# Turning the second half's attention probabilities by 64-row products, behind the whole dense sum, with half of the probabilities in the norm tile

## The chip, the cores and the metric

The kernel runs on one core of one Trainium2 chip. The metric is the device time in microseconds (us) of one execution. The engines are named as in the profile: PE is the matmul engine (TensorE), PEld its weight load, DVE the vector engine, ACT the scalar engine, POOL the GpSimd engine, SP the engine that issues most DMAs.

## The reference

Four layers stand one behind the other on a sequence of 2048 tokens of width 512: a recurrent attention layer A, a dense layer B, A again, B again, each with a residual sum and a layer norm ahead of it. In short:

```python
def attention(x, mem0):                     # A, 32 heads of 128
    mem = mem0                              # 8 memory rows
    for s in range(64):                     # segments of 32 tokens
        h = concat(mem, x[32*s:32*s+32])    # 40 rows
        q, k, v = h @ Wq, h @ Wk, h @ Wv    # per head
        scores = where(mask, q @ k.T * 128**-0.5, -1e9)
        o = (softmax(scores) @ v) @ Wo      # summed over the heads
        mem = o[:8]                         # carried to the next segment
        out[s] = o[8:]

x = x + attention(layernorm(x), mem0)
x = x + relu(layernorm(x) @ w1) @ w2        # B, inner width 1376
x = x + attention(layernorm(x), mem0)
x = x + relu(layernorm(x) @ w1) @ w2
```

Weights and inputs are bf16. The recurrence makes the segments of one attention layer strictly sequential.

## The kernel before

**Steps.** The program is a row of 68 steps, `step(k)` for k = 1 to 67 behind `first_step()` (k = 0). In step k the first attention layer (a = 0) works on segment k and the second attention layer (a = 1) on segment k - 4; from k = 4 to 63 both are active ("two-layer steps", 60 of them), in the others one ("single" steps: 0 to 3 and 64 to 67). The dense layer of a segment pair runs inside the later steps as `dense_h` (first product and ReLU) and `dense_y` (second product, "the dense sum", accumulated in the PSUM bank `sp_banks[1]`).

**Order.** PE, DVE, SP and POOL run in the order in which the program is written (`tc.manual_schedule`); ACT's order is made by a planner. PE and DVE take their instructions strictly in that order, so a product or a copy that must wait holds up all that stands behind it on its engine. The framework puts in the semaphore waits, from the tiles that an instruction reads and writes.

**A step.** With L = 40 rows per layer, the 32 heads are worked in two halves (`hf` = 0, 1) of 16. For each half: queries and keys (`qk`, L591, evicted from PSUM by L597 on ACT and L599 on DVE), scores (L625) into `sp`, and `softmax`: maximum (L643), difference (L647), exponential (L649, on ACT), sum (L659), reciprocal (L660) and the product with it (L664), which writes the probabilities. A row of the probability tile is (head parity g, query), a column (head pair, layer, key). To be multiplied with the values they have to be turned, keys onto partitions.

- Half 0 lies in `P_sb` and is turned by a transposing DMA into `PT0` (`turn_p`, L682).
- Half 1 lies in `P1_sb` and is turned on PE by `transpose_p(1, cut)`: for each of 8 head pairs and each layer a product of all 128 rows, 64 columns of `P1_sb` held, 80 columns of the identity moving (L675), into two PSUM tiles `tp`. The first tile (`cut` = 5 pairs in two-layer steps, 4 in single ones) is copied to `PT_sb` by ACT, the second by DVE (L679).

After it come `weighted_v` (L701, 64 small products of a 40-row value block with the turned probabilities, the first 32 of them with half 0), the copies of its result to `OTm` (memory rows) and `OTx` (tokens) (`outputs`, L719), the product of the memory rows with `Wo` (`output_mem`, L633), the new memory (L849, L857, L868, L872), values of the next step (L354, L797).

**Around the change.** In a two-layer step the order on PE behind the second half's scores is: filling work (`dense_h`, `block`), `dense_y(k-2, 0, 9)` (18 products), `transpose_p(1, 5)` (16), `dense_y(k-2, 9, 11)` (4), `weighted_v`, `output_mem`. On DVE it is: sums, reciprocals and L664 of the second half, `add_output(k-1)` (two sums into the residual, L379; in every fourth step there is none, and a short piece of the input's moments, L220 and L221, may stand in its place), then the copy of the second `tp` (L679), then the copies L719.

**The norm tile.** `XN` (128 x 512, bf16) takes the normalised rows at the end of a step (L227). A transposing DMA (`transpose_step`, L291) turns it into `xnT` early in the next step; nothing else reads it, but for the last rows of the program.

Of the kernel before, what the change touches and what calls it, by code (L numbers as in the profile page):

```python
# [7 lines left out]
BF = mybir.dt.bfloat16  # L8
F32 = mybir.dt.float32
ALU = mybir.AluOpType  # L10
# [12 lines left out]
def kernel(  # L23
# [14 lines left out]
    nc = tc.nc  # L38
    _, S, Dm = A_x.shape
    _, H, Dh = A_Wq.shape[0], A_Wq.shape[1], A_Wq.shape[2]  # L40
# [4 lines left out]
    L = M + SEG  # L45
    NSEG = S // SEG
    assert NSEG % 4 == 0 and DELTA == 4
    LAST = NSEG + DELTA - 1
    NXT = NSEG // 4
    NC4 = Dm // 128  # L50
    NFC = (Dff + 127) // 128
# [5 lines left out]
    const = ctx.enter_context(tc.tile_pool(name="const", bufs=1))  # L57
    wk = ctx.enter_context(tc.tile_pool(name="wk", bufs=2))
    dram = ctx.enter_context(tc.tile_pool(name="vdram", bufs=2, space=DRAM))
    ps_c = ctx.enter_context(tc.tile_pool(name="ps_c", bufs=3, space=PSUM))  # L60
# [11 lines left out]
    def has1(k):  # L72
        return DELTA <= k <= LAST
# [22 lines left out]
    def span(d):  # L96
        offs = ([0] if has0(d) else []) + [o for o, _ in slots_of.get(d, [])]
        return base(d) + min(offs), base(d) + max(offs) + 32
# [65 lines left out]
    ident = const.tile([128, 128], BF)  # L164
# [3 lines left out]
    ident_q = ident[:].rearrange("p (g q) -> p g q", g=2)[:, :, 0:L]  # L168
# [22 lines left out]
    XN = const.tile([128, Dm], BF)  # L191
# [3 lines left out]
    Vs = const.tile([128, H * Dh], BF)  # L195
    P_sb = const.tile([128, 8, 128], BF)
    nc.gpsimd.memset(P_sb[:], 0.0)
    P1_sb = const.tile([128, 16 * L + 24], BF)
    nc.gpsimd.memset(P1_sb[:], 0.0)
    PT_sb = const.tile([128, 8, 2, L], BF)  # L200
    PT0 = const.tile([128, 8, 128], BF)
    OTx = const.tile([128, H, 64], BF)
# [6 lines left out]
    for a in range(2):  # L209
        t = ps_s.tile([128, 512], F32, name=f"sp{a}")  # L210
# [24 lines left out]
    def moments_x(n):  # L235
        return stat_tail(stats_x(n), "x")
# [295 lines left out]
    def dense_y(d, f0, f1, bank=1):  # L532
        if not 0 <= d <= LAST:
            return
        lo, hi = span(d)
        n = hi - lo
        for fc in range(NFC)[f0:f1]:
            fs = 128 if fc < NFC - 1 else F_LAST
            for j in range(2):


                w = 8 * L if fc == 0 else 256
                nc.tensor.matmul(sp_banks[bank][64 * j:64 * j + n, 0:w], lhsT=hT_tiles[d][0:fs, fc, 0:n],  # L543
                                 rhs=w2_flat[0:fs, fc * Dm + 256 * j:fc * Dm + 256 * j + w],
                                 start=(fc == 0), stop=(fc == NFC - 1), skip_group_check=True,
                                 tile_position=(0, 64 * j))
# [68 lines left out]
    def masks(*act):  # L615
        for a in act:
            nc.vector.tensor_copy(out=sp_tiles[a], in_=maskb2)  # L617
# [20 lines left out]
    def exponentials(act):  # L638
        mxs, ess = {}, {}
        for a in act:  # L640
            sp = sp_tiles[a]
            mxs[a] = wk.tile([128, 8], F32, tag="mx", bufs=2, name="mx")
            nc.vector.tensor_reduce(out=mxs[a][:], in_=sp, axis=AX.X, op=ALU.max)  # L643
        for a in act:
            sp = sp_tiles[a]
            es = ess[a] = wk.tile([128, 8, L], F32, tag="es", bufs=2, name="es")
            nc.vector.tensor_tensor(out=es[:], in0=sp, in1=mxs[a][:].unsqueeze(2).to_broadcast([128, 8, L]),  # L647
                                    op=ALU.subtract)
            last_exp[0] = nc.scalar.activation(out=es[:], in_=es[:], func=ACTF.Exp, scale=SCALE)  # L649
        return ess  # L650

    def softmax(hf, act, by_pe=False, ess=None):
        if ess is None:
            ess = exponentials(act)
        if by_pe and hf:
            transpose_p(0)
        for a, es in ess.items():
            sm = wk.tile([128, 8], F32, tag="sm", bufs=2)
            nc.vector.tensor_reduce(out=sm[:], in_=es[:], axis=AX.X, op=ALU.add)  # L659
            nc.vector.reciprocal(out=sm[:], in_=sm[:])  # L660
            eng = nc.vector if by_pe or (hf, a) == (1, act[-1]) else nc.gpsimd
            P = P1_sb[:, 0:16 * L].rearrange("p (s a q) -> p s a q", s=8, a=2)[:, :, a, :] if hf else \
                P_sb[:, :, 64 * a:64 * a + L]
            eng.tensor_tensor(out=P, in0=es[:],  # L664
                              in1=sm[:].unsqueeze(2).to_broadcast([128, 8, L]), op=ALU.mult)

    def transpose_p(hf, cut=4):

        for s0, ns, copy in ((0, cut, nc.scalar.copy), (cut, 8 - cut, nc.vector.tensor_copy)):
            tp = ps_c.tile([128, ns, 2, L], F32, tag="c", name="tp")  # L670
            for sl in range(ns):
                for a in range(2):
                    c = L * (2 * (s0 + sl) + a)
                    P = P1_sb[:, c:c + 64] if hf else P_sb[:, s0 + sl, 64 * a:64 * a + 64]
                    nc.tensor.matmul(tp[64 * a:64 * a + 64, sl], lhsT=P, rhs=ident_q,  # L675
                                     start=True, stop=True, tile_position=(0, 64 * a))
            PT = PT_sb[:, s0:s0 + ns] if hf else \
                PT0[:, s0:s0 + ns].rearrange("p s (g q) -> p s g q", g=2)[:, :, :, 0:L]
            copy(out=PT, in_=tp[:])  # L679

    def turn_p():
        nc.sync.dma_start_transpose(out=PT0[:], in_=P_sb[:].rearrange("p s k -> p (s k)"))  # L682
# [3 lines left out]
    def weighted_v(act):  # L686
        pvs = {}
        for t, (h0, nh) in enumerate(PVS):
# [6 lines left out]
            for hi in range(nh):  # L695
                hf, hh = divmod(h0 + hi, 16)
                sl, g2 = divmod(hh, 2)
                for a in act:
                    R = 64 * a
                    PT = PT_sb[R:R + L, sl, g2, :] if hf else PT0[R:R + L, sl, 64 * g2:64 * g2 + L]  # L700
                    nc.tensor.matmul(pvs[t, a][:, hi, :], lhsT=Vs[R:R + L, (h0 + hi) * Dh:(h0 + hi + 1) * Dh],  # L701
                                     rhs=PT, start=(hi == 0 or (t, a) != (1, 1)), stop=True,
                                     skip_group_check=(t, a) == (1, 1))
# [181 lines left out]
    def first_step():  # L885


        slots = iter([w1_flat[:, 512 * i:512 * i + 512] for i in range(NC4 * Dff // 512)] +
                     [w2_flat[:, 512 * i:512 * i + 512] for i in range(8)])
        masks(0)  # L890
        with tc.high_priority(offset=PRIO):
            qks = qk(0, [0])
            scores(qks, [0])
            softmax(0, [0], True)
            values_first(0)
            memory_values(0, (next(slots), None), (0,))
            values_second(0, next(slots))
            values0(1, 0, stage=next(slots))
            values0(1, 2, stage=next(slots))
            m = moments_x(2)  # L900
            normalize(nc.vector, xbs[2], xbs[2], m, 0, 128)
            inputs_T(2)
            values0(3, 0, stage=next(slots))
            values0(3, 2, stage=next(slots))
            load_x(1)
            qks = qk(1, [0], between=lambda: values0(5, 0, stage=next(slots)))
            scores(qks, [0])
            softmax(1, [0], True)
            values0(5, 2, stage=next(slots))
            values_first(1)  # L910
            memory_values(0, (None, next(slots)), (1,))
            transpose_p(1)
            tokens_in(1)
            nc.gpsimd.tensor_copy(out=HTm[:, :, 2 * M:32], in_=spare_T(1))
            values_second(1, next(slots))
            pvs = weighted_v([0])
            outputs(0, pvs)
            wo = ps_wo.tile([128, Dm], F32, tag="wo", name="wo")
            for groups, heads in zip((((1, 4),), ((1, 6),), ((3, 4),), ((3, 6), (5, 4)), ()), WO_PARTS):
                for p, n in groups:  # L920
                    values0(p, n, stage=next(slots))
                output_mem(0, wo, *heads)
            new_memory(0, [0], wo)
            output_ride(0)
            prepare(1)
# [7 lines left out]
    def step(k):  # L933
        act = layers(k)
        single = len(act) == 1
# [4 lines left out]
        ahead = has1(k + 1) or not cont  # L940
# [65 lines left out]
        else:  # L1006
# [1 line left out]
                evict_behind.append(last_exp[0].ins)  # L1008
            block(k, part, H)
            evict_behind.clear()  # L1010
        f_mid = 9 if ahead or k == 2 else 5
        if k < LAST:
            dense_y(k - 2, 0, f_mid)
        if not single:
# [5 lines left out]
        elif not single and k % 4 == 1 and has_x:  # L1020
            mom["x"] = stat_tail(mom["stats"], "x")
        with tc.high_priority(offset=PRIO):
            transpose_p(1, 4 if single else 5)
        if ahead and k < LAST:
            dense_y(k - 2, f_mid, NFC)
        tokens_in(k + 1)
        if k < LAST and spare_T(k + 1) is not None:
            nc.gpsimd.tensor_copy(out=HTm[:, :, 2 * M:32], in_=spare_T(k + 1))
# [11 lines left out]
        if cont:  # L1040
            with tc.high_priority(offset=PRIO):
                pool, tag = (ps_c, "c") if single else (ps_wo, "wo")
# [24 lines left out]
    with tc.manual_schedule(engines={mybir.EngineType.PE, mybir.EngineType.DVE, mybir.EngineType.SP,  # L1067
                                   mybir.EngineType.Pool}):
        load_rest()
        tp = transpose_pe(mem0)  # L1070
# [21 lines left out]
        R = residual(d)  # L1092
        t = xnT_tiles[d + 2] = wk.tile([128, NC4, 128], BF, tag="xnT", bufs=1, name="xnT")
# [8 lines left out]
        for fc in order:  # L1102
            fs = 128 if fc < NFC - 1 else F_LAST
            for q in range(4):
                u, j = divmod(q, 2)
                nc.tensor.matmul(sp_banks[0][32 * q:32 * q + 32, 0:256], lhsT=hT_tiles[d][0:fs, fc, SEG * u:SEG * u + SEG],  # L1106
                                 rhs=w2_flat[0:fs, fc * Dm + 256 * j:fc * Dm + 256 * j + 256],
                                 start=(fc == order[0]), stop=(fc == order[-1]), tile_position=(0, 32 * q))
        ob = wk.tile([128, 256], BF, tag="xb", bufs=1, name="ob")
        nc.vector.tensor_tensor(out=ob[:], in0=R[:, 0:256], in1=sp_banks[0][:, 0:256], op=ALU.add)  # L1110
        for u in range(2):
            r = S - SEG * (u + 1)
            for j, queue in ((0, nc.sync), (1, nc.scalar)):
                q = 64 * u + 32 * j
# [36 lines left out]
```

## Time and profile before

| what | value |
|---|---|
| runs | 1577.96, 1580.86, 1581.55 us; median 1580.86 us |
| profiled execution | span 1580.0 us from the first to the last instruction; the page gives no other time of it |
| busy, share of the span | PE 98%, PEld 81%, DVE 81%, ACT 47%, POOL 22% |
| granted PE clock | 1.000 |
| mean length of a two-layer step | 23.09 us |

The span of the profiled execution is 0.86 us below the median of the runs, so the two can be compared nearly without a correction. In the rows of the profile, "L675" is line 675 of the kernel, `out<-in` are the program's names with numbers left out (`P_sb` stands for `P1_sb` as well), x16 is a number of instructions, and `[0.75 <-ACT HTm L868]` is idle time of the engine ahead of the row and what ended it. A matmul's duration (some 0.18 us) is its latency; products follow each other at a far shorter distance, which is read from the starts of rows.

### The profile page before, as it was taken

How to read it: one execution, taken by the hardware profiler on the slowest of the kernel's cores; microseconds unless marked ns; L12 is line 12 of the kernel's file. 1: busy time of each engine (PE TensorE's matmuls, PEld its weight loads, DVE VectorE, ACT ScalarE, POOL GpSimd, SP SyncE). 2: the span in 40 equal slices, each digit the busy share in tenths (PEclk: the TensorE clock that was granted, in tenths of full speed). 3: DMA queues.
4: the chain of work that ended last, by engine and by line, in shares of the span. 5: the costliest groups of instructions: out<-in, count | busy, mean ns of one | idle time of the engine just before them, and what ended most of it. 6: DMA issues, size and time to landing. Idle time of an engine off the chain costs nothing. (4 is left out here: it accounts for less than half of the span.)

```text
span 1580.0 us, 95139 instructions
## 1 busy us (share of the span) xinstructions
PE 1548.6 (98%) x42866; PEld 1286.3 (81%) x42866; DVE 1277.3 (81%) x3300; ACT 734.7 (47%) x1762; POOL 349.8 (22%) x670
## 2 busy tenths in 40 slices
PE   5899999999999999999999999999999999999998
PEld 3677888888888888888888888988888898888876
DVE  3578888888888888888888888888888888887866
ACT  3435445454544545454454545445454544545433
POOL 2012122222222222222122222212222221222110
PEclk9999999999999999999999999999999999999999
DMA  9734432434353244434433343443443344333331
GB/s 369 246 77 76 87 84 78 81 92 79 78 92 84 78 82 94 80 76 91 84 80 80 99 80 76 88 84 79 77 99 77 72 87 80 82 74 95 75 69 41
DMA packets 222021, 146.26 MB, mean 93 GB/s; under 512 B 123464, under 2 KB 215984, under 8 KB 221616
## 3 DMA queue, kind: packets, MB, share of 16 engines
q1 hardware_dynamic: 218448, 135.96, 38.8%
q8 instruction: 336, 5.51, 1.5%
q0 software_dynamic: 3072, 4.20, 1.1%
q14 instruction: 69, 0.57, 0.1%
q10 hardware_dynamic: 96, 0.03, 0.0%
HBM read 65.41 MB, written 45.35 MB: 70 GB/s over the span
## 5 line engine op out<-in xcount | busy, mean ns | idle before, releaser
L597 ACT CAST QT<-qp 128x480 bf16<-128x480 f32 (+3 forms) x408 | 201.5, 494 | 433.4 <-PE qp L591 433.1
L591 PE MATMUL qp<-HT,Wq_sb 128*128 128x80 bf16 (+1 forms) x8704 | 371.3, 200 | 3.2 <-POOL HT L786 1.2
L591 PEld LDWEIGHTS <-Wq_sb 128*128 128x128 bf16 x8704 | 325.9, 100 | 35.2 <-issue 27.5
L591 PE MATMUL qp<-HT,Wk_sb 128*128 128x80 bf16 (+1 forms) x8704 | 347.3, 199 | 1.7 <-issue 1.3
L591 PEld LDWEIGHTS <-Wk_sb 128*128 128x128 bf16 x8704 | 319.5, 100 | 2.6 <-issue 1.6
L664 POOL TENSOR_TENSOR P_sb<-es,sm 128x320 bf16<-128x320 f32 x185 | 130.8, 721 | 714.8 <-ACT QT L597 299.4
L599 DVE CAST KT<-qp 128x480 bf16<-128x480 f32 (+3 forms) x408 | 220.3, 565 | 36.3 <-PE qp L591 32.9
L643 DVE TENSOR_REDUCE mx<-sp 128x8 f32<-128x320 f32 x256 | 115.1, 487 | 133.1 <-PE sp L625 130.9
L373 PE MATMUL wox<-Wo_sb,OTx 128*64 128x256 bf16 x2880 | 173.6, 273 | 0.0
L373 PEld LDWEIGHTS <-OTx 128*64 128x64 bf16 x2880 | 150.2, 110 | 2.9
L649 ACT ACTIVATE es<-es 128x320 f32<-128x320 f32 x256 | 109.5, 468 | 61.9 <-DVE es L647 61.0
L797 PE MATMUL vm<-Wv_sb,HTm 128*32 128x512 bf16 x2176 | 129.4, 379 | 1.8 <-DVE KT L599 1.0
L354 PE MATMUL v<-Wv_sb,xnT 128*32 128x512 bf16 x2048 | 128.8, 378 | 0.0
L633 PE MATMUL wo<-Wo_sb,OTm 128*32 128x512 bf16 x2144 | 128.6, 380 | 0.0
L659 DVE TENSOR_REDUCE sm<-es 128x8 f32<-128x320 f32 x256 | 117.4, 459 | 13.5 <-ACT es L649 5.0
L617 DVE CAST sp<-maskb 128x320 f32<-128x320 bf16 x256 | 118.3, 483 | 0.0
L647 DVE TENSOR_TENSOR es<-sp,mx 128x320 f32<-128x320 f32 x256 | 113.6, 482 | 1.5
L543 PE MATMUL sp<-w_sb,hT 128*64 128x256 bf16 (+4 forms) x1452 | 103.9, 276 | 0.4 <-issue 0.4
L522 PE MATMUL hp<-xnT,w_sb 128*128 128x64 bf16 (+1 forms) x2948 | 98.5, 192 | 0.9 <-issue 0.5
L801 ACT CAST VmS<-vm 128x512 bf16<-128x512 f32 x134 | 78.5, 586 | 44.4 <-PE vm L797 42.5
L222 POOL TENSOR_TENSOR mv<-mv,mhalf_t 128x1 f32<-128x1 f32 x82 | 45.8, 558 | 224.6 <-DVE mv L221 218.9
L797 PEld LDWEIGHTS <-HTm 128*32 128x32 bf16 x2176 | 54.7, 97 | 48.8 <-issue 3.1
(125 smaller groups left out, 2088.5 us busy)
## 6 DMA issues: line engine op xcount, KB each, us to landing
Vs<-vd SPq DMA_DIRECT2D x96, 256.0 KB
vd<-vst SPq DMA_DIRECT2D x181, 128.0 KB
vmd<-VmS SPq DMA_DIRECT2D x134, 128.0 KB
Vs<-vmd SPq DMA_DIRECT2D x254, 32.0 KB
Vs<-vmd SPq DMA_DIRECT2D x60, 128.0 KB
Wq_sb<-in_A_Wq_dram SPq DMA_DIRECT2D x2, 2048.0 KB
Wk_sb<-in_A_Wk_dram SPq DMA_DIRECT2D x2, 2048.0 KB
Wv_sb<-in_A_Wv_dram SPq DMA_DIRECT2D x2, 2048.0 KB
```

The lines of the kernel that those rows point to most:

```text
L354: nc.tensor.matmul(vp[32 * j:32 * j + 32, :], lhsT=tokens[:, c4, :], rhs=Wv_sb[:, c4, n * 512:(n + 1) * 512], start=(c4 == 0), stop=(c4 == ...
L373: nc.tensor.matmul(out[64 * j:64 * j + nr, 0:256], lhsT=lhsT, rhs=rhs[:, 256 * j:256 * j + 256], start=start, stop=stop, tile_position=(0, ...
L591: nc.tensor.matmul(qp[:, hi, 0:ncol], lhsT=W_sb[:, c4, h * Dh:(h + 1) * Dh], rhs=HT[:, c4, a_lo:a_hi, :], start=(c4 == 0), stop=(c4 == NC4 ...
L597: nc.scalar.copy(out=dst[:, 0:nh, a_lo * L:a_hi * L], in_=qp[:, 0:nh, 0:ncol])
L599: nc.vector.tensor_copy(out=dst[:, 0:nh, a_lo * L:a_hi * L], in_=qp[:, 0:nh, 0:ncol])
L617: nc.vector.tensor_copy(out=sp_tiles[a], in_=maskb2)
L633: nc.tensor.matmul(wo[32 * j:32 * j + 32, :], lhsT=OTm[:, h, n, 2 * M * c:2 * M * c + 4 * M], rhs=Wo_sb[:, h, :], start=(h < 4), stop=(h > ...
L643: nc.vector.tensor_reduce(out=mxs[a][:], in_=sp, axis=AX.X, op=ALU.max)
L647: nc.vector.tensor_tensor(out=es[:], in0=sp, in1=mxs[a][:].unsqueeze(2).to_broadcast([128, 8, L]), op=ALU.subtract)
L659: nc.vector.tensor_reduce(out=sm[:], in_=es[:], axis=AX.X, op=ALU.add)
L664: eng.tensor_tensor(out=P, in0=es[:], in1=sm[:].unsqueeze(2).to_broadcast([128, 8, L]), op=ALU.mult)
L797: nc.tensor.matmul(vp[32 * j:32 * j + 32, :], lhsT=HTm[:, c4, :], rhs=Wv_sb[:, c4, n * 512:(n + 1) * 512], start=(c4 == 0), stop=(c4 == NC ...
```

## The change

- The second half's probabilities are laid out as 4 head pairs of 104 columns (layer 0 in columns 0 to 39, layer 1 in 64 to 103) in each of two tiles: pairs 0 to 3 (u = 0) in the norm tile `XN`, pairs 4 to 7 (u = 1) in `P1_sb`. The product L664 of this half becomes two products of 128 x 160 per layer, on the same engine as before (POOL for layer 0 of a two-layer step, else DVE).
- `transpose_p(1, cut)` is replaced by `turn_second`: for u, pair and head parity g a product over the 64 rows of that g, 104 columns held, 40 columns of the identity moving, so that both layers come out at once. The result of g lies in PSUM tile `tps[g]`. Behind the 8 products of u = 0, ACT copies `tps[0]`'s and DVE `tps[1]`'s columns of u = 0 to `PT_sb`, then the 8 products of u = 1 go into the other columns of the same two tiles, and are copied in the same way.
- All 22 products of the dense sum stand ahead of the turn, where 4 of them stood behind it (in steps 3 to 66).

```diff
-    P1_sb = const.tile([128, 16 * L + 24], BF)
+    PW1 = 64 + L
+    P1_sb = const.tile([128, 4 * PW1], BF)
     nc.gpsimd.memset(P1_sb[:], 0.0)
+    P1 = [t[:, 0:4 * PW1].rearrange("p (s k) -> p s k", s=4) for t in (XN, P1_sb)]
...
             eng = nc.vector if by_pe or (hf, a) == (1, act[-1]) else nc.gpsimd
-            P = P1_sb[:, 0:16 * L].rearrange("p (s a q) -> p s a q", s=8, a=2)[:, :, a, :] if hf else \
-                P_sb[:, :, 64 * a:64 * a + L]
-            eng.tensor_tensor(out=P, in0=es[:],
-                              in1=sm[:].unsqueeze(2).to_broadcast([128, 8, L]), op=ALU.mult)
+            if not hf:
+                eng.tensor_tensor(out=P_sb[:, :, 64 * a:64 * a + L], in0=es[:],
+                                  in1=sm[:].unsqueeze(2).to_broadcast([128, 8, L]), op=ALU.mult)
+                continue
+            for u in range(2):
+                eng.tensor_tensor(out=P1[u][:, :, 64 * a:64 * a + L], in0=es[:, 4 * u:4 * u + 4],
+                                  in1=sm[:, 4 * u:4 * u + 4].unsqueeze(2).to_broadcast([128, 4, L]), op=ALU.mult)
+
+    def turn_second():
+
+        tps = [ps_c.tile([128, 8, L], F32, tag="c", name="tp") for _ in range(2)]
+        for u in range(2):
+            for sl in range(4):
+                for g in range(2):
+                    R = 64 * g
+                    nc.tensor.matmul(tps[g][0:PW1, 4 * u + sl, :], lhsT=P1[u][R:R + 64, sl, :],
+                                     rhs=ident[R:R + 64, R:R + L], start=True, stop=True)
+            for g, copy in ((0, nc.scalar.copy), (1, nc.vector.tensor_copy)):
+                copy(out=PT_sb[0:PW1, 4 * u:4 * u + 4, g, :], in_=tps[g][0:PW1, 4 * u:4 * u + 4, :])
...
-        f_mid = 9 if ahead or k == 2 else 5
+        f_mid = NFC if ahead else 9 if k == 2 else 5
         if k < LAST:
             dense_y(k - 2, 0, f_mid)
...
         with tc.high_priority(offset=PRIO):
-            transpose_p(1, 4 if single else 5)
-        if ahead and k < LAST:
-            dense_y(k - 2, f_mid, NFC)
+            turn_second()
         tokens_in(k + 1)
```

`transpose_p` itself stays, without its `hf` and `cut`, for the first half of the three steps that turn it on PE (0, 1 and 67).

More of the change, by code (lines that the diff above doesn't have):

```diff
@@ L655, in softmax @@
         if by_pe and hf:
-            transpose_p(0)
+            transpose_p()
         for a, es in ess.items():
@@ L661, in softmax @@
             eng = nc.vector if by_pe or (hf, a) == (1, act[-1]) else nc.gpsimd
-            P = P1_sb[:, 0:16 * L].rearrange("p (s a q) -> p s a q", s=8, a=2)[:, :, a, :] if hf else \
-                P_sb[:, :, 64 * a:64 * a + L]
-            eng.tensor_tensor(out=P, in0=es[:],
-                              in1=sm[:].unsqueeze(2).to_broadcast([128, 8, L]), op=ALU.mult)
[L667 to L671, printed above, removed]
+            if not hf:
+                eng.tensor_tensor(out=P_sb[:, :, 64 * a:64 * a + L], in0=es[:],
+                                  in1=sm[:].unsqueeze(2).to_broadcast([128, 8, L]), op=ALU.mult)
+                continue
@@ L672, in transpose_p @@
+    def transpose_p():
+        for s0, copy in ((0, nc.scalar.copy), (4, nc.vector.tensor_copy)):
+            tp = ps_c.tile([128, 4, 2, L], F32, tag="c", name="tp")
+            for sl in range(4):
                 for a in range(2):
-                    c = L * (2 * (s0 + sl) + a)
-                    P = P1_sb[:, c:c + 64] if hf else P_sb[:, s0 + sl, 64 * a:64 * a + 64]
-                    nc.tensor.matmul(tp[64 * a:64 * a + 64, sl], lhsT=P, rhs=ident_q,
+                    nc.tensor.matmul(tp[64 * a:64 * a + 64, sl], lhsT=P_sb[:, s0 + sl, 64 * a:64 * a + 64], rhs=ident_q,
@@ L676, in transpose_p @@
                                      start=True, stop=True, tile_position=(0, 64 * a))
-            PT = PT_sb[:, s0:s0 + ns] if hf else \
-                PT0[:, s0:s0 + ns].rearrange("p s (g q) -> p s g q", g=2)[:, :, :, 0:L]
-            copy(out=PT, in_=tp[:])
+            copy(out=PT0[:, s0:s0 + 4].rearrange("p s (g q) -> p s g q", g=2)[:, :, :, 0:L], in_=tp[:])
     def turn_p():
@@ L911, in first_step @@
             memory_values(0, (None, next(slots)), (1,))
-            transpose_p(1)
+            turn_second()
             tokens_in(1)
@@ L1022, in step @@
         with tc.high_priority(offset=PRIO):
-            transpose_p(1, 4 if single else 5)
-        if ahead and k < LAST:
-            dense_y(k - 2, f_mid, NFC)
+            turn_second()
         tokens_in(k + 1)
```

## The prediction

> **What bounds the kernel now.** I read the page first, then the timeline of one two-layer step around the turn, then the same distances for all 60 of them, then the groups by shape, and last the tiles that two engines share.
>
> ```profile
> PE 1548.6 (98%) x42866; PEld 1286.3 (81%) x42866; DVE 1277.3 (81%) x3300; ACT 734.7 (47%) x1762; POOL 349.8 (22%) x670
> ```
>
> PE is busy 98% of the span at a granted clock of 1.000; its 31 us of idle time lie mostly at the two ends of the run. In the middle a step is a gapless row of products, so an added wait on PE costs its full length in every step, and a product saved gains its distance to the next one. The timeline around one turn:
>
> ```profile
> 818.33 0.71 POOL L664 TENSOR_TENSOR P_sb<-es,sm 128x320 bf16<-128x320 f32 x1 [3.74 <-DVE sm L660]
> ...
> 818.55 1.18 PE L543 MATMUL sp<-w_sb,hT 128*64 128x320 bf16 x18
> 818.77 0.63 DVE L664 TENSOR_TENSOR P_sb<-es,sm 128x320 bf16<-128x320 f32 x1
> 819.43 0.85 DVE L379 TENSOR_TENSOR R<-R,wox 64x256 f32<-64x256 f32 x2
> 819.56 0.46 PE L675 MATMUL tp<-ident,P_sb 128*64 128x80 bf16 x16
> 819.85 0.39 PE L543 MATMUL sp<-w_sb,hT 128*64 128x256 bf16 x4
> 819.95 0.49 ACT L679 CAST PT_sb<-tp 128x400 bf16<-128x400 f32 x1 [2.17 <-PE tp L675]
> 820.17 0.49 PE L701 MATMUL pv<-PT,Vs 40*128 40x40 bf16 x25
> 820.31 0.41 DVE L679 CAST PT_sb<-tp 128x240 bf16<-128x240 f32 x1
> ...
> 820.59 0.18 PE L701 MATMUL pv<-PT_sb,Vs 40*128 40x40 bf16 x1
> ...
> 820.67 0.73 DVE L719 CAST OTm<-pv 128x96 bf16<-128x96 f32 x3
> ...
> 821.08 0.61 PE L633 MATMUL wo<-Wo_sb,OTm 128*32 128x512 bf16 x8
> ```
>
> From the starts: the 16 products of the turn take 0.29 us of PE, the 4 of the dense sum 0.32, the 64 of L701 0.91 with the hand-over to L633. The last 4 dense products and the 32 products with half 0 (820.17 to 820.59) cover the copies of `tp`: ACT's ends at 820.44, DVE's, late because the sums L379 keep DVE until 820.28, at 820.72, and it is first needed at the 21st product with half 1, about 820.84. No PE time is lost here today.
>
> The rows that price the new operations:
>
> ```profile
> L599 DVE CAST KT<-qp 128x160 bf16<-128x160 f32 x16 | 5.0, 315 | 0.1
> L597 ACT CAST QT<-qp 128x160 bf16<-128x160 f32 x16 | 4.7, 293 | 17.1 <-PE qp L591 17.1
> L701 PE MATMUL pv<-PT_sb,Vs 40*128 40x40 bf16 x1536 | 37.3, 177 | 0.0
> ```
>
> And one place where two engines share a PSUM tile, in a single step (timeline):
>
> ```profile
> 1512.95 0.27 PE L857 MATMUL mt<-sel,wm 128*32 128x16 bf16 x16
> 1513.66 0.19 ACT L868 CAST HTm<-mt 128x32 bf16<-128x32 f32 x1
> 1513.88 0.19 DVE L872 CAST HT<-mt 128x32 bf16<-128x32 f32 x1 [0.75 <-ACT HTm L868]
> ```
>
> Both only read `mt`, and write different tiles; yet DVE, idle for 0.75 us, waits for ACT's end and starts 0.03 us later. The view of L872 has this wait 5 times of 5, and where DVE copies first (all two-layer steps), ACT starts 0.10 to 0.14 us behind DVE's end in all 60. So accesses of different engines to one PSUM bank are put one after the other here, even where the data would not ask for it.
>
> **The change, part by part.** Times run from the start of the new turn, T'.
>
> *Dense sum moved.* The 4 products cost the same 0.32 us ahead of the turn, so T' is 0.32 us later than the old start (819.88 in the step shown). The probabilities are ready earlier than that (DVE's L664 ends at 819.40). Nothing is gained or lost on PE, but the cover behind the turn is gone: its price stands below.
>
> *Turn's products.* 16 of 40 moving columns over 64 rows, alternating between row halves, for 16 of 80 columns. Nearest rows: L701 (64 such alternating products in 0.81 us, 12.6 ns each) and L625 (32 products of 40 columns in about 0.5 us, 16 ns). So 0.20 to 0.27 us; I take 0.20, as L701 has the same row split. Gain 0.08 us a step, at most; at the other end 0.02.
>
> *Probabilities in two pieces.* DVE's 128x320 product takes 0.63 us. For two halves the bounds are nothing more, or one more fixed part: casts of 160 and 320 columns (315 and 485 ns) leave 145 ns fixed. Neighbours on DVE overlap by 20 to 90 ns, so I take +0.10, between 0 and 0.14. It delays `add_output` and the copies behind it in DVE's queue, not the turn. On POOL the one product (0.71 us) becomes two; even at twice the time it ends at 819.77, before T'. Behind it stand the token copies (L786, L1028), which the next step needs 6 us later: nothing. `XN` was last read by the transposing DMA that feeds `dense_h`, whose products ran 4 us before, and is next written at the end of the step: nothing.
>
> *The wait inside the turn.* The products of u = 1 write the same two PSUM tiles, other columns, that ACT and DVE are reading for u = 0. By the `mt` rows PE must wait for both copies. The 8th product starts at T'+0.09 and its data are there at +0.27 (177 ns). ACT is idle (2.17 us before its copy now), starts at +0.31, and ends at +0.60. DVE's copy takes 0.315 us and starts at +0.32 if DVE is free, else behind `add_output`. In the step shown add_output ended 0.72 us behind the old turn's start, so at 0.72 - 0.32 + 0.10 = +0.50; copy from +0.53 to +0.84; PE goes on at +0.89 (0.05 us is what PE takes behind DVE in the rows of `P_sb` and `KT`). In steps where it ended at 0.59 the same sum gives +0.77, where there is no `add_output` +0.69. Then 0.10 for u = 1, and L701 starts at +0.99, +0.87 or +0.79, against +0.29 today (820.17 less 819.88). So 0.70, 0.58 and 0.50 us a step. 28 steps are of the first kind, 13 of the second, some 15 of the third, the rest between; applied to the recorded end of DVE's work in each of the 60, the mean is 0.61 us. The turn's 0.08 is in this.
>
> *Behind the turn.* The copies of u = 1 end 0.65 us after PE resumes on them; L701 needs them 0.70 us after: no further wait. DVE's first copy L719 then ends at about 0.90, and L633 follows it by 0.14: 1.04, against 1.01 if L701 alone set it: +0.02 a step.
>
> *Single steps.* The same wait with DVE free costs about 0.4 us in each of 8, but in one (1527) L701 already waits 0.9 us for the DMA of `PT`, and hides it: 2.8 us.
>
> Sum: 60 x 0.63 + 2.8 = 40.6 us. On the execution's 1580.0 us that is 1620.6; carried to the median of the runs, 1621 us. Low end: P halves free, nothing behind the turn, 60 x 0.54 + 2 = 34.5, so 1615. High end: P halves at +0.14, 16.7 ns a product, a release that takes 0.15 us (the distance from DVE's L719 to L633), 0.1 us behind: 60 x 0.88 + 4 = 57, so 1638.
>
> *Two rules of the Trainium skill.* "PSUM — Partial Sum Buffer", section "PSUM bank collisions raise a hardware error", says that a PE write and a read by ACT or DVE in one bank and the same partitions collide even at disjoint columns, and that software has to keep them apart; this speaks against the change, and by it neither of the first two rivals below could happen. The `mt` rows show such keeping apart for two readers; no row shows it for a PE write. "TensorE: Matmul & The Clock Gate", section "LDWEIGHTS (loading the stationary operand)", makes a weight load's time its columns over 1.2: 87 ns for 104 columns, 53 for 64. By it the sum would be up to 33 us larger (16 x 34 ns x 60), if loads were exposed. The trace doesn't bear it out: 128x64 loads take 111 ns, 40x128 loads 93 ns.
>
> **The rivals.** *Copies only late, no wait inside the turn*: if the framework lets u = 1 run beside the copies, L701 starts at +0.21 and meets its first product with half 1 of g = 1 at +0.61, when DVE's copy is at +0.84, +0.72 or +0.65. With the release and the late L719 copies behind them this costs 0.28, 0.15 and 0.08 us: about 12 us, 1593. For it: probabilities of the two layers are written into one SBUF tile by POOL and DVE at the same time (818.33 and 818.77), so disjoint parts are told apart there. Against it: `mt`.
>
> *Faster*: the same, and L701 never waits. That is 60 x 0.075, 4.5 us less, 1576. It decides from where both copies of u = 0 are done by +0.56, and DVE's of u = 1 by +0.8. ACT's alone ends at +0.60 by its row and DVE's, when free, at +0.64, so it would need copies a fifth faster and DVE free of L379.
>
> *Loads exposed*: the turn's loads don't overlap, at 93 ns each (L701's loads) for 16 instead of 12.6: 1.3 us a step, 77 us on top, 1698. Against it: L701's 64 loads of 128 columns lie inside 0.81 us.
>
> *It doesn't do what it says*: the turn's products are no shorter (0.27), and the waits are covered by later slack, so the time stays. Against it: PE has no idle time in the steps that could take up 0.6 us.
>
> **How the numbers follow.** The forecast has 0.86, late copies alone 0.07, faster 0.03, exposed loads 0.02, no change 0.02. A measurement of this kernel can tell about 0.2%, 3.2 us, from no change. Faster is thus 0.03, same 0.02, slower 0.95. The forecast's own range is 1615 to 1638; to hold 8 in 10 with its unknown sizes it is stretched down to the late-copies case: 1592 to 1638.
>
> **What would show it.** In the profile after: the 16 products of the turn in two groups of 8, 0.6 to 0.8 us apart, with PE idle between them, released by L679 of DVE (in most steps) or ACT; some 0.5 us of idle PE at each turn; a two-layer step of 23.7 us instead of 23.09; four L679 copies a step near 0.3 us; L701 behind the turn without a wait. Wrong: the second group right behind the first (then the late copies, seen as waits at L701's products with `PT_sb`), or loads of 104 columns that push the products to 50 ns and more apart.

## The result and the profile after

The changed kernel takes 1639.86 us (median of 5 runs, 1638.81 to 1641.69) against 1580.86 us before: a ratio of 1.0377, 95% interval 1.0364 to 1.0389. That is 59 us more, where 40 were forecast, and 1.9 us above the end of the range. The profiled execution took 1638.81 us, with a span of 1637.1 us, 57.1 more than the span before, at the same granted clock of 1.000. The page of after:

```profile
PE 1579.0 (96%) x42866; PEld 1317.0 (80%) x42866; DVE 1305.6 (80%) x3436; ACT 741.8 (45%) x1830; POOL 358.6 (22%) x730
```

PE has as many instructions as before, but is now idle for 58 us instead of 31. The view of the waits says at what (us in total, times, longest):

```profile
PE tp L679 <- ACT PT_sb L682: 25.8, 68, 0.6
```

L679 is the turn's product, L682 its copies: 68 waits, one in each step, that were not there before. The same turn as the one shown of before, in the timeline of after:

```profile
846.02 0.44 POOL L669 TENSOR_TENSOR XN<-es,sm 128x160 bf16<-128x160 f32 x1 [3.80 <-DVE sm L662]
846.40 0.33 DVE L669 TENSOR_TENSOR XN<-es,sm 128x160 bf16<-128x160 f32 x1
846.44 0.60 POOL L669 TENSOR_TENSOR P_sb<-es,sm 128x160 bf16<-128x160 f32 x1
846.64 0.57 DVE L669 TENSOR_TENSOR P_sb<-es,sm 128x160 bf16<-128x160 f32 x1
...
847.25 0.85 DVE L381 TENSOR_TENSOR R<-R,wox 64x256 f32<-64x256 f32 x2
847.51 0.37 PE L679 MATMUL tp<-ident,XN 64*104 64x40 bf16 x8
847.91 0.29 ACT L682 CAST PT_sb<-tp 104x160 bf16<-104x160 f32 x1 [2.49 <-PE tp L679]
848.14 0.33 DVE L682 CAST PT_sb<-tp 104x160 bf16<-104x160 f32 x1
848.26 0.58 PE L679 MATMUL tp<-ident,P_sb 64*104 64x40 bf16 x8 [0.38 <-ACT PT_sb L682]
848.68 0.55 PE L714 MATMUL pv<-PT,Vs 40*128 40x40 bf16 x25
...
848.90 0.32 DVE L682 CAST PT_sb<-tp 104x160 bf16<-104x160 f32 x1 [0.44 <-PE tp L679]
...
849.24 0.56 DVE L732 CAST OTm<-pv 128x96 bf16<-128x96 f32 x2
...
849.64 0.40 PE L635 MATMUL wo<-Wo_sb,OTm 128*32 128x512 bf16 x4
```

The two groups of 8 are 0.75 us apart. The first product of the second group starts 0.05 us behind ACT's copy, the second one, at 848.51, 0.05 us behind DVE's (848.14 + 0.33), which came late because the residual sums L381 kept DVE until 848.10. From the turn's start to L635 it is 2.13 us, where the step before had 1.52 with 4 products of the dense sum inside. Two steps' lengths, from turn to turn, before and after (the first two numbers of a row, window and length):

```profile
819.56:842.65 23.09, 23.09 (x651) 19.80 (x648) 19.61 (x51) 10.60 (x25) 5.34 (x11) 1.00 0.37 82
842.65:865.73 23.08, 23.08 (x651) 19.81 (x648) 19.27 (x50) 10.59 (x25) 5.35 (x11) 1.00 0.38 82
```

```profile
847.51:871.66 24.15, 23.69 (x649) 20.24 (x648) 20.15 (x53) 10.75 (x26) 5.46 (x12) 1.00 0.45 78
871.66:895.56 23.90, 23.52 (x649) 20.23 (x648) 19.70 (x52) 10.69 (x26) 5.47 (x12) 1.00 0.45 80
```

For the account I took the starts of the rows in all 60 two-layer steps and averaged the **stage** from the first product of the dense sum to the first of the output product (L633, here L635):

| kernel | to the turn | turn, first to last product | to the first value product | to the output product | stage |
|---|---|---|---|---|---|
| before | 1.025 | 0.259 | 0.360 | 0.916 | 2.56 us |
| after | 1.326 | 1.050 | 0.045 | 1.000 | 3.42 us |

60 x 0.861 = 51.7 us of the 57.1 lie in this stage. From the first query product of one step to that of the next, the two-layer steps last 23.07 us in the mean before (the 23.09 given above is the median) and 23.95 after, so some 1.5 us lie in the rest of these steps and 3.9 in the single steps with the start and the end. A price of its own for keeping half of the probabilities in the norm tile can't be seen: the rest of a two-layer step is only 0.025 us longer.

### The profile page after: what moved, and what is told of

Read it like the earlier page. It is cut to its first block, busy times and chain, and to the rows that moved or that the text cites. A ratio compares the mean times of both kernels' runs of the same rounds, so it can differ in the third digit from the quotient of the medians.

```text
span 1637.1 us, 95522 instructions
## 1 busy us (share of the span) xinstructions
PE 1579.0 (96%) x42866; PEld 1317.0 (80%) x42866; DVE 1305.6 (80%) x3436; ACT 741.8 (45%) x1830; POOL 358.6 (22%) x730
## 4 chain that ended last, share of the span: by engine, by line
PE 86%; DVE 7%; issue 3%; ACT 2%; DMA 2%; SPq 1%; POOL 0%; POOLq 0%
PE qp L593 37%; PE wo L635 7%; PE vm L810 7%; PE v L356 7%; PE hp L524 5%; PE wox L375 5%; PE vp L312 3%; PE pv L714 3%; PE sp L627 3%; PE sp L545 3%; PE tp L679 2%; DVE sm L661 2%; DMA Wv_sb<-in_A_Wv_dram 2%; DVE R L381 1%; DVE P_sb L669 1%
## 5 line engine op out<-in xcount | busy, mean ns | idle before, releaser
L665 POOL TENSOR_TENSOR P_sb<-es,sm 128x320 bf16<-128x320 f32 x125 | 87.8, 722 | 501.3 <-ACT QT L599 317.3
L635 PE MATMUL wo<-Wo_sb,OTm 128*32 128x512 bf16 x2144 | 128.5, 380 | 0.0
L682 ACT CAST PT_sb<-tp 104x160 bf16<-104x160 f32 x136 | 39.8, 293 | 176.8 <-PE tp L679 176.8
L568 POOL COPY R<-R 32x512 f32<-32x512 f32 x62 | 37.6, 607 | 267.8 <-issue 263.1
L810 PEld LDWEIGHTS <-HTm 128*32 128x32 bf16 x2176 | 58.4, 97 | 46.8 <-issue 3.9
```

The costliest lines, as they stand in the source:

```text
L635: nc.tensor.matmul(wo[32 * j:32 * j + 32, :], lhsT=OTm[:, h, n, 2 * M * c:2 * M * c + 4 * M], rhs=Wo_sb[:, h, :], start=(h < 4), stop=(h > ...
L810: nc.tensor.matmul(vp[32 * j:32 * j + 32, :], lhsT=HTm[:, c4, :], rhs=Wv_sb[:, c4, n * 512:(n + 1) * 512], start=(c4 == 0), stop=(c4 == NC ...
```

## The experiments

Theory B, the prediction's: PE stands in the turn because the second group writes PSUM banks that the copies of the first are reading. Rival C: what costs is the lost cover of the copies; without that wait, PE would stand as long at the value products. The first four kernels part these two, and try the width of the loads; the four after them the terms that were mis-sized; the last three close the account.

**128 held columns** (`e1_w128`): 

```diff
-    PW1 = 64 + L
+    PW1 = 128
...
-                copy(out=PT_sb[0:PW1, 4 * u:4 * u + 4, g, :], in_=tps[g][0:PW1, 4 * u:4 * u + 4, :])
+                copy(out=PT_sb[0:64 + L, 4 * u:4 * u + 4, g, :], in_=tps[g][0:64 + L, 4 * u:4 * u + 4, :])
```

> The changed kernel with 128 instead of 104 held columns per product of the turn (the 24 more are not copied). Theory W (the turn's products stand 24.5 ns apart instead of the forecast 12.6 because a load of 104 columns is slow, one of 128 columns quick as in the value products): 16 products at about 12.6 ns; where DVE is held by the residual sums until 0.5 to 0.6 us the first 8 are absorbed, so 0.1 us is saved in 43 steps and 0.2 in 17: about 8 us less than the changed kernel, 1630 to 1633. Rival R (the distance comes from the 64 rows or from two PSUM banks in turn): the distance stays 24.5 ns and the time 1639 to 1640.

Measured 1638.39 us, ratio to before 1.0360 (1.0345 to 1.0376): not to be told from the changed kernel. The groups by shape (last numbers ahead of the second bar: busy us, mean ns of one), first of after, then of this one:

```profile
L679 PEld LDWEIGHTS <-P_sb 64*104 64x104 bf16 x544 | 30.3, 122 | 34.5 <-issue 30.4
```

```profile
L679 PEld LDWEIGHTS <-P_sb 64*128 64x128 bf16 x544 | 21.8, 93 | 42.4 <-issue 40.2
```

Theory W is right on the distance and wrong on the time. A pair of products (one for each g) follows the last at 25 ns instead of 49, a load takes 93 ns instead of 122; but of the expected 8 us only some 1.5 came, which the spread of the runs covers (the profiled stage is 1.7 us shorter in 60 steps). This kernel also puts the pairs 128 columns apart in the tile instead of 104. That the held width decides and not this distance, two rows of the kernel before speak for: pieces of 64 columns that lie 64 apart load slowly, pieces of 128 quickly.

```profile
L373 PEld LDWEIGHTS <-OTx 128*64 128x64 bf16 x2880 | 150.2, 110 | 2.9
...
L701 PEld LDWEIGHTS <-Vs 40*128 40x128 bf16 x4096 | 59.3, 93 | 14.3 <-issue 14.0 <-DMA xT<-xb 0.2
```

In steps with late residual sums the first group's 0.1 us vanishes in the wait for DVE, as expected. The second group's 0.05 us vanishes too: the first value product starts that much sooner, but the stream of them behind it does not (below).

**Copies behind all the products** (`e2_copies_behind`):

```diff
                     nc.tensor.matmul(tps[g][0:PW1, 4 * u + sl, :], lhsT=P1[u][R:R + 64, sl, :],
                                      rhs=ident[R:R + 64, R:R + L], start=True, stop=True)
+        for u in range(2):
             for g, copy in ((0, nc.scalar.copy), (1, nc.vector.tensor_copy)):
```

> The changed kernel with all 16 products of the turn ahead of its four copies. Theory B (PE waits between the two groups of 8 only because the second group writes the two PSUM banks that ACT and DVE are reading): no gap in the turn, value products with the second half start behind 0.1 to 0.2 us of wait for DVE's copies, 0.35 to 0.5 us less a step: 1609 to 1616. Rival C (the time is the lost cover of the copies; without the wait in the turn PE waits as long at the value products): 1633 to 1640, with the idle time of PE moved to L714.

Measured 1602.06 us, ratio 1.0132 (1.0116 to 1.0147): 38 us less than the changed kernel, by one line that puts the copies into a loop of their own. Timeline:

```profile
875.75 0.37 PE L679 MATMUL tp<-ident,XN 64*104 64x40 bf16 x8
875.96 0.35 PE L679 MATMUL tp<-ident,P_sb 64*104 64x40 bf16 x8
876.15 0.48 PE L715 MATMUL pv<-PT,Vs 40*128 40x40 bf16 x25
876.34 0.48 ACT L683 CAST PT_sb<-tp 104x160 bf16<-104x160 f32 x2 [2.69 <-PE tp L679]
876.38 0.56 DVE L683 CAST PT_sb<-tp 104x160 bf16<-104x160 f32 x2
876.69 0.19 PE L715 MATMUL sp<-PT_sb,Vs 40*128 40x40 bf16 x1
```

The turn has no gap, and the wait has not moved: the value products run on, with about 0.1 us lost ahead of the first with half 1. Theory B holds and C falls as the main cost. The rows also show from the other side that accesses to one bank are put one after the other: ACT's first copy reads columns whose products had started by 875.94 and are done some 0.2 us later, yet it starts at 876.34, behind the last product into the same bank.

**Four dense products behind the turn again** (`e3_dense_behind`):

```diff
-        f_mid = NFC if ahead else 9 if k == 2 else 5
+        f_mid = 9 if ahead or k == 2 else 5
...
             turn_second()
+        if ahead and k < LAST:
+            dense_y(k - 2, f_mid, NFC)
```

> The changed kernel with the last 4 products of the dense sum behind the turn again, as before the change. Theory B: the wait is inside the turn and ends with DVE's copy, which is bound by the residual sums at the same absolute time in 43 steps, so the 4 products come on top of it: no gain, some 0.1 to 0.25 us a step slower, 1643 to 1653. Rival C (lost cover): the cover is back, some 0.3 us a step less, 1620 to 1625.

Measured 1668.08 us, ratio 1.0543 (1.0525 to 1.0561), 28 us slower than the changed kernel. The sign is B's; the size was expected smaller. The stage is 3.71 us, 17 us more in 60 steps. The rest of the 28 lies outside it, where steps are 0.25 us longer in the profile. The granted clock was 0.990 to 0.993 in the four runs of this kernel, and 0.997 to 1.000 in those of all the others; this fits longer steps outside the stage, but why it was lower here stays open. Between the turn's last product and the first value product stand 0.47 us, of which four dense products at the usual 53 ns make 0.21.

**The whole dense sum ahead, in the kernel before** (`e4_dense_ahead`):

```diff
-        f_mid = 9 if ahead or k == 2 else 5
+        f_mid = NFC if ahead else 9 if k == 2 else 5
...
             transpose_p(1, 4 if single else 5)
-        if ahead and k < LAST:
-            dense_y(k - 2, f_mid, NFC)
```

> The kernel before with only the move of the 4 dense products ahead of the turn (old products, old layout, old copies). Theory B: this alone costs the wait of the value products for ACT's first copy and the later start of DVE's memory copies, 0.1 to 0.2 us a step: 1587 to 1593. Rival C (lost cover is the main cost): 1615 or more. If the cover is free: 1580 to 1582.

Measured 1588.94 us, ratio 1.0048 (1.0033 to 1.0063): the lost cover alone costs 8 us, as expected of B.

**Probabilities in one piece** (`e5_one_piece`):

```diff
-    XN = const.tile([128, Dm], BF)
-    nc.vector.memset(XN[:], 0.0)
+    PW1 = 64 + L
+    XNP = const.tile([128, 8 * PW1], BF)
+    nc.vector.memset(XNP[:], 0.0)
+    XN = XNP[:, 0:Dm]
...
-    P1 = [t[:, 0:4 * PW1].rearrange("p (s k) -> p s k", s=4) for t in (XN, P1_sb)]
+    P1 = XNP[:].rearrange("p (s k) -> p s k", s=8)
...
-            for u in range(2):
-                eng.tensor_tensor(out=P1[u][:, :, 64 * a:64 * a + L], in0=es[:, 4 * u:4 * u + 4], ...)
+            eng.tensor_tensor(out=P1[:, :, 64 * a:64 * a + L], in0=es[:], ...)
```

> The changed kernel with the second half's probabilities in one piece again: one tile of 8 x 104 columns whose first 512 columns are the norm tile, one product of 128x320 per layer instead of two of 128x160. Theory H (the two halves hold DVE some 0.18 us longer, not the forecast 0.10, and by that the residual sums and DVE's first PT copy): PE goes on inside the turn 0.18 us earlier in the 28 steps with the late sums, 0.07 in 13, the same in the rest: 6 us less than the changed kernel, 1633 to 1635. If the halves cost 0.10: 1636. If they cost nothing or PE waits for something else: 1639 to 1640.

Measured 1634.09 us, ratio 1.0333 (1.0317 to 1.0348): 5.8 us less, theory H's size. The groups of DVE's two halves in after:

```profile
L669 DVE TENSOR_TENSOR P_sb<-es,sm 128x160 bf16<-128x160 f32 x68 | 37.0, 544 | 0.0
...
L669 DVE TENSOR_TENSOR XN<-es,sm 128x160 bf16<-128x160 f32 x68 | 22.3, 328 | 2.3
```

These means include the eight single steps. In the two-layer steps the halves take 0.33 and 0.57 us, and 0.82 from the first's start to the second's end; the one piece takes 0.68 here and took 0.63 before. The residual sums end 0.46 us behind the turn's start here, 0.60 in after.

The trace also shows what holds DVE. In the single steps, where POOL has no such product beside it, the halves take 0.56 us from first start to last end and the one piece 0.49. In the two-layer steps DVE's last product ends at a fixed distance behind POOL's, 0.35 us with one piece (in the kernel before, `e4`, `e5` and `e6`) and 0.18 with halves (in after and `e2`), in each of the 60 steps to within 0.01 us. It has started by then (846.64 above, where POOL's ends at 847.04), so it is not a wait for POOL ahead of it. POOL's own two halves take 1.02 us from first start to last end, where its one piece took 0.71.

**The halves alone, in the kernel before** (`e8_halves_alone`): 

```diff
-            eng.tensor_tensor(out=P, in0=es[:],
-                              in1=sm[:].unsqueeze(2).to_broadcast([128, 8, L]), op=ALU.mult)
+            for s0, s1 in ((0, 4), (4, 8)) if hf else ((0, 8),):
+                eng.tensor_tensor(out=P[:, s0:s1], in0=es[:, s0:s1],
+                                  in1=sm[:, s0:s1].unsqueeze(2).to_broadcast([128, s1 - s0, L]), op=ALU.mult)
```

> The kernel before, with only the second half's probability product made in two pieces of 128x160 per layer, in the old tile and layout. Theory H: DVE's work behind it is 0.18 us later, its PT copy ends at 1.34 us behind the turn's start instead of 1.16 in 28 steps, the memory copies and the output product 0.1 to 0.17 us later there, less in the others: 1584 to 1587. Rival: DVE's work is covered, 1580 to 1582.

Measured 1592.26 us, ratio 1.0061 (1.0049 to 1.0074): H's sign, and 10 us, more than expected. Timeline:

```profile
822.39 0.86 POOL L665 TENSOR_TENSOR P_sb<-es,sm 128x160 bf16<-128x160 f32 x2 [3.75 <-DVE sm L660]
...
822.83 0.93 DVE L665 TENSOR_TENSOR P_sb<-es,sm 128x160 bf16<-128x160 f32 x2
...
823.62 0.53 PE L676 MATMUL tp<-ident,P_sb 128*64 128x80 bf16 x16
```

DVE's two take 0.93 us and end 0.14 us behind the turn's first product, so here PE waits for them as well.

**The value products' waits ahead** (`e7_waits_first`):

```diff
-    def turn_second():
+    def turn_second(act=()):
...
         tps = [ps_c.tile([128, 8, L], F32, tag="c", name="tp") for _ in range(2)]
+        for a in act:
+            R = 64 * a
+            nc.tensor.matmul(tps[a][:, 0, :], lhsT=Vs[R:R + L, 0:Dh], rhs=PT0[R:R + L, 0, 0:L], start=True, stop=True)
...
-            turn_second()
+            turn_second(() if single else act)
```

> The changed kernel with two more products ahead of the turn in two-layer steps, which read the values and the first half's turned probabilities and whose results are written over by the turn. Theory Q (behind the wait in the turn, the value products start 0.15 us late because their own semaphore waits, on transfers long landed, stand in PE's queue behind the waiting product and are worked off only then): these waits are worked off ahead, value products run 0.05 to 0.1 us sooner behind PE's release, less 0.03 to 0.05 for the two products: 1635 to 1639. Rival: the late start is the switch between products or loads, nothing is gained, and the two products cost 0.05 us a step: 1641 to 1643.

Measured 1631.98 us, ratio 1.0314 (1.0300 to 1.0328): 8 us less for two products more, beyond theory Q's own size; 5.8 of them lie in the stage (3.32 us), and where the other 2 lie stays open. The weight loads of after, then of this kernel:

```profile
848.26 0.48 PEld L679 LDWEIGHTS <-P_sb 64*104 64x104 bf16 x7 [0.44 <-issue]
848.63 0.44 PEld L714 LDWEIGHTS <-Vs 40*128 40x128 bf16 x22
```

```profile
844.44 0.46 PEld L682 LDWEIGHTS <-P_sb 64*104 64x104 bf16 x7 [0.44 <-issue]
844.80 0.59 PEld L717 LDWEIGHTS <-Vs 40*128 40x128 bf16 x39
```

Both rows end with their view's window, so only their rates can be compared: from start to start the 22 loads of after follow each other at 17 ns in the mean (0.09 us of it between the first and the second), the 39 here at 13. From the first value product to the first with half 1 it is 0.40 us in all 60 steps, instead of 0.47 in most and up to 0.63 in the others. In after two wait instructions a step stand in PE's queue between the turn and the value products (from the view of L714: count, then shortest, median and longest in ns):

```profile
L714 PEldq EVENT_SEMAPHORE  x127: 51/51/51, 66.9 to 1622.6; - x127
```

In the step shown they start 0.015 and 0.14 us behind PE's release, not before it, and the stream of value products begins only behind them. In `e7` these waits stand at the two added products, 0.75 us sooner and ahead of the turn, and PE doesn't stand there: the transfers had landed.

**Three repairs together** (`e6_one_piece_w128_behind`: `e5` with `PW1 = 128` and the copies of `e2`):

> All three repairs together: probabilities in one piece in a joined tile, 128 held columns, all 16 products of the turn ahead of the four copies. Theory B with W and H: turn 0.20 us, copies ready by 0.76 to 1.02 us behind its start in all steps, value products wait some 0.1 us, 0.15 us less a step than the kernel with only the copies behind (1602): 1590 to 1595, still slower than the kernel before by what the lost cover costs. Rival F (the 64-row products themselves are a gain once the waits are gone): below 1580.

Measured 1590.24 us, ratio 1.0048 (1.0034 to 1.0062). The turn's products take 0.19 us from first to last, where the old ones took 0.26; the stage is 2.70 us against 2.56 before. Rival F falls: the new form with its waits gone is as slow as the old one without its cover (`e4`).

**All terms but the order of the copies** (`e9_all_but_order`: `e5` with `PW1 = 128` and the two products of `e7`):

> The changed kernel with the three mis-sized terms mended and the wait in the turn left as it is: 128 held columns, probabilities in one piece in a joined tile, the value products' waits worked off ahead by two more products. If the three terms are all that the forecast of 1621 had wrong: the sum of their single runs, 15 us less than the changed kernel, 1625, or down to 1618 where the quick loads count now that the value products no longer start late. If something else is missing: above 1629.

Measured 1618.69 us, ratio 1.0234 (1.0219 to 1.0249), 21 us less than the changed kernel, the lower end of what was expected: the single savings of `e1`, `e5` and `e7` make 15. Here the value products can use the quick distance of the second group: from PE's release to the output product it is 1.00 us, against 1.07 in `e7`.

**All four** (`e10_all_four`: `e6` with the two products of `e7`) and **three with dense behind** (`e11_three_dense_behind`: `e6` with the edit of `e3`):

> All repairs and the copies behind: the kernel of the three repairs (1590) with the value products' waits worked off ahead. There PE doesn't stand in the turn, so its waits are worked off while the dense sum runs and nothing is to be gained: 1590 to 1593, with 0.03 us a step for the two products. If those waits cost there too: 1583 to 1586.

> The kernel of the three repairs (1590) with the last 4 products of the dense sum behind the turn again. Theory S (going from whole-row products to 64-row products and back costs PE some 0.1 us each time beyond the products, and this order has two more such changes, which take up what the cover gives): 1588 to 1596. Rival C (cover is all that is missing): 8 us less, 1581 to 1584.

Measured 1589.47 us (1.0059, 1.0042 to 1.0076) and 1588.82 us (1.0047, 1.0032 to 1.0062); both can't be told from `e6`. So where PE does not stand in the turn, the queued waits cost nothing that the runs can tell (`e10`), and theory S holds against rival C (`e11`). In `e11` the four dense products with what surrounds them take 0.45 us between turn and value products, 0.36 in the kernel before, and the way into the turn is again 0.21 us from the last dense product, 0.12 before. So some 0.18 us a step goes into the two changes between whole-row and 64-row products that this order has more than the kernel before, and the cover is used up by them. No version of the new form beat the kernel before.

## Why the prediction was wrong

The mechanism stands as forecast: two groups of 8 with PE idle between them, four copies near 0.3 us, the wait ended by DVE behind its residual sums in most steps. What failed is the size, 0.86 us a step in place of 0.63: three terms of the sum were mis-sized, the turn's products, the probabilities in two pieces, and the way behind the turn. Step by step:

- *Dense sum moved*: forecast 0.32 us later start of the turn; 0.30. The number is right, in part by luck: ahead of the old turn the four products cost 0.21 us (`e4`), and the other 0.09 is a longer way from the last dense product into the new turn, 0.20 us instead of 0.12, which the forecast did not have. The cover lost was priced through the wait; alone it costs 8 us (`e4`).
- *Turn's products*, 12.6 ns each "as L701 has the same row split": **wrong**. They came at 24.5 ns; the turn's own products are slower than the old ones, no 0.08 us gained. L701 shares the row split but holds 128 columns, the turn 104, and that decides (`e1`). The first group's data so came 0.1 us later, which moved the wait's end in the steps without residual sums (0.81 us behind the turn's start, forecast 0.69). By itself it is worth some 1.5 us, within the spread of the runs.
- *Probabilities in two pieces*, +0.10 on DVE, bounds 0 to 0.14: **wrong, outside the bounds**. The halves hold DVE for 0.82 us against 0.63, 0.19 more (0.05 of it stays with one piece in the new layout, `e5`, and why is open). The fixed part came from casts that ran alone, and alone it holds: 0.07 more in the single steps. In the two-layer steps DVE's end follows POOL's, and POOL's halves take 0.30 us more than its one piece. The forecast had put these at nothing, because they end before T'; what they cost came back through DVE. PE's release came at 1.00 and 0.88 us instead of 0.89 and 0.77. Worth 5.8 us (`e5`).
- *The wait inside the turn*: right in place, cause and length once the two terms above are put in. Taking it away gave 38 us (`e2`). The `mt` rows, two readers of one bank, led to the right forecast for a write behind a read.
- *Behind the turn*, 1.04 us from PE's release to L633: **wrong**, 1.13 in most steps and 1.24 to 1.33 in 12 of the 60. I let L701 start 0.10 us behind the release at full rate; with its queued waits it reached that rate only at 0.25. Worth 8 us (`e7`), 5.8 of them in the stage.
- *Single steps*: 2.8 forecast; 3.9 measured, with the start and the end of the run.

With these three terms mended and the wait left in, the kernel takes 1618.7 us (`e9`), where the forecast for that wait was 1621: nothing large is missing in the sum. The two are not quite the same kernel. In `e9` the halves cost nothing where the forecast had 0.10 us, some 4 us by its own steps, and the two added products cost 0.04 us a step, 2.4 us; these estimates cancel in part. The high end of the range, 1638, was made from other things (a later release, slower products); it lacked a bound for DVE products that end behind POOL's and one for PE's queue after a stall.

Of the rules weighed: the Trainium skill's page "PSUM — Partial Sum Buffer", section "PSUM bank collisions raise a hardware error", fits the trace: PE's write was kept behind the reads of other columns in the same bank. What would come of a collision no run shows. The rule of the Trainium skill's section "LDWEIGHTS (loading the stationary operand)", columns over 1.2, does not fit: 104 columns took 122 ns and 128 columns 93. The Trainium skill's page "TensorE: Matmul & The Clock Gate" has, in the section "Weight-path perf modes — Fast Weight Load (FWL) and DoubleRow", the rule that I missed: the quick load is on when the number of weights is 128. The 49 and 25 ns a pair agree with it.

## What to carry to other kernels

Where products and copies share a PSUM bank, write all products into it before the first copy out of it, or give the groups banks of their own (not tried here): a finer split of the copies that is meant to start them sooner can put a wait on PE instead, and here that was 38 of 59 us. Price a small product from a row with the same held width, not only the same rows; price a split instruction beside the other engine's instruction that runs at the same time, and with that one split too. After a stall of PE, count the waits queued behind the stall as well, and let an earlier instruction meet them.

## What the runs showed of the hardware

- Held columns: 64-row products with 104 held columns follow each other at 24.5 ns, with 128 at 12.6 ns; the loads take 122 and 93 ns. In the kernel before, loads of 64 columns take 110 ns.
- Two DVE products of 128x160 beside POOL's: 0.33 and 0.57 us, 0.82 from first start to last end (0.93 in `e8`); alone, in the single steps, 0.33 and 0.32, 0.56 in all. One of 128x320: 0.49 us alone, beside POOL's 0.63 (before) and 0.68 (`e5`), with its end 0.35 us behind POOL's. The Trainium skill's "SBUF — State Buffer", section "SBUF: two separate sides", has DVE and GpSimd block each other on a shared pair of ports; the durations beside POOL's, in the single steps without it, and the fixed distance of the ends fit that.
- Going from whole-row to 64-row products costs about 0.2 us from start to start, where dense products follow each other at 0.05 and the old turn follows them at 0.12. The Trainium skill's "TensorEngine Tiling (Array Packing)", section "Key Properties", says that a change of the tiling mode drains the engine; the rows fit that, though no run parts a drain from other causes.
